# A hand-ordered opening for the first layer of a transformer stack: loads, norms, transposes, warm-up matmuls and zero fills

## The chip, the cores and the metric

The kernel runs on one core of one Trainium2 chip. The metric is the device time of the slowest (here the only) core in microseconds, us. Lower is better. A run of a one-core program is called fast when it lies within 1.5% of the fastest run of the same kernel. Runs of one kernel differ mostly by 1 to 2 us (about 0.1%). The changes discussed here are 1 to 8 us, so two measures stand side by side throughout: the time over several runs, and one instant read from the trace, at which the opening is over.

## The reference, cut to what matters

Two layers alternate, twice each: a sliding dilated attention (A) and a token-mixing MLP (B), on 2048 rows of 1024 columns in bf16.

```python
x = x + A(layernorm(x), wqkv, wo)      # first A: the part that the change touches
x = x + B(layernorm(x), w1, b1, w2, b2)
x = x + A(layernorm(x), wqkv, wo)
x = x + B(layernorm(x), w1, b1, w2, b2)
```

The first A begins with a layer norm of x, then `q, k, v = layernorm(x) @ wqkv`. The kernel computes v first ("the V matmuls": 16 row tiles x 2 column halves x 8 = 256 matmuls of 512 columns), then q and k ("the K/Q matmuls"). The biases b1 (3584 values) and b2 (2048 values) are wanted only by the first B, hundreds of us later.

## The kernel before

Each of the 16 row tiles is loaded, normed on VectorE (two half statistics, an aggregate, a rsqrt on ScalarE, the norm) and turned to its transpose hT, because the matmul wants the contraction on the partitions. The first four tiles are transposed by TensorE and copied by ScalarE; the others by DMA. Nobody orders the engines' queues by hand here: the code is traced in program order, and a scheduler decides the order of each engine's queue by what it believes will be ready first.

```python
def load_biases():
    with nc.allow_non_contiguous_dma(reason="tiny bias loads"):
        nc.gpsimd.dma_start(out=b1_bf[:], in_=B_b1.rearrange("(t p) -> p t", p=P))
        nc.gpsimd.dma_start(out=b2_bf[:], in_=B_b2.rearrange("(i m c) -> m i c", m=P, c=DIL))
    nc.vector.tensor_copy(out=b1_sb[:], in_=b1_bf[:])     # "the cast of b1"
    nc.vector.tensor_copy(out=b2_sb[:], in_=b2_bf[:])
...
for t in qT:                                              # zero fills, on GpSimd
    nc.gpsimd.memset(t[:, S:S + PAD], 0.0)
for t in Pm:
    nc.gpsimd.memset(t[0:HK, :, :, HW:KW], 0.0)
    nc.gpsimd.memset(t[HK:P, :, :, 0:HK], 0.0)
...
def prologue(c, i, on_pe):
    ...
    nc.sync.dma_start(out=x, in_=xin_v[c, i])
    yield
    mean, rs = stats(x, 1.0, eps1)
    norm_dve(x, x, mean, rs)
    if on_pe:
        tp = pss.tile([P, KD, P], BF16, name="s", tag="s")
        for kt in range(KD):
            nc.tensor.transpose(tp[:, kt, :], x[:, kt * P:(kt + 1) * P], ident[:])
        nc.scalar.copy(out=hT[:, :, cols(c, i)], in_=tp[:])
    else:
        nc.sync.dma_start_transpose(out=hT[:, :, cols(c, i)], in_=x)
    yield
...
    if first:
        pro = [prologue(c, i, c == 0 and i < 4) for c, i in order]
        ...                                               # loads of x and wv, interleaved
        wts = load_qk(0)
        load_biases()
        for k in range(4):
            next(pro[k])
            v_proj(v, *order[k], wv, (0,))
        ...                                               # other norms, other V matmuls
```

The cast turns the bf16 biases into the fp32 that later instructions want. b1 is read so that partition p gets elements p, p + 128, p + 256 and so on, which is 3584 separate pieces of 2 bytes; b2 is 1024 pieces of 4 bytes.

The softmax here doesn't subtract the row's maximum and nothing guards it: scores larger than these inputs give would overflow.

Of the kernel before, what the change touches and what calls it, by code (L numbers as in the profile page):

```python
# [9 lines left out]
ACT = mybir.ActivationFunctionType  # L10
ALU = mybir.AluOpType
FP32 = mybir.dt.float32
BF16 = mybir.dt.bfloat16

P = 128
# [10 lines left out]
def kernel(  # L26
# [15 lines left out]
    nc = tc.nc  # L42
    x_in = A_x[0]
    out2d = out[0]
    S, D = x_in.shape
    F = B_w1.shape[1]
    KD = D // P
    FT = F // P
    NT = S // P
# [4 lines left out]
    NDC = D // 512  # L54
    FB = 256
    NFB = F // FB
    GF = FB // P
    NW2 = 4
    HF = FT // NW2
    KW = P + W  # L60
    HK = P // 2
    HW = HK + W
    PAD = W
    SHIFT = 14.0
    assert D == H * DH and NT == 16 and NI == 8 and NG == 8 and HG == 4
    scale = float(DH) ** -0.5

    def pool(name, bufs, **kw):
        return ctx.enter_context(tc.tile_pool(name=name, bufs=bufs, **kw))
# [5 lines left out]
    gop = pool("gop", NFB)  # L75
# [5 lines left out]
    pss = pool("pss", 2, space=bass.MemoryType.PSUM)  # L81
    psa = pool("psa", 1, space=bass.MemoryType.PSUM)

    def m_tile():
        return psm.tile([P, 512], FP32, name="m", tag="m")
# [16 lines left out]
    def x2(name, shape=None, dt=BF16):  # L102
        return x2p.tile(shape or [P, D], dt, name=name, tag="x2")
# [4 lines left out]
    def st(name, shape):  # L108
        return stat.tile(shape, FP32, name=name, tag=name)
# [5 lines left out]
    ident = const.tile([P, P], BF16, name="ident")  # L115
    make_identity(nc, ident[:])
    eps1 = const.tile([P, 1], FP32, name="eps1")
# [20 lines left out]
# [4 lines that stand above are left out]
        nc.vector.tensor_copy(out=b1_sb[:], in_=b1_bf[:])  # L142
        nc.vector.tensor_copy(out=b2_sb[:], in_=b2_bf[:])

    hT = pers.tile([P, KD, S], BF16, name="hT")
    qT = [pers.tile([P, S + PAD], BF16, name=f"qT{n}") for n in range(2)]
    kT = [pers.tile([P, S], BF16, name=f"kT{n}") for n in range(2)]
    Pm = [pers.tile([P, HG, NI, KW], BF16, name=f"Pm{n}") for n in range(2)]
    for t in qT:
        nc.gpsimd.memset(t[:, S:S + PAD], 0.0)  # L150
    for t in Pm:
        nc.gpsimd.memset(t[0:HK, :, :, HW:KW], 0.0)
        nc.gpsimd.memset(t[HK:P, :, :, 0:HK], 0.0)

    xa = [dram.tile([S, D], BF16, name=f"xa{li}") for li in range(2)]
    xb = dram.tile([S, D], BF16, name="xb")
# [1 line left out]
    xin_v = x_in.rearrange("(i p c) d -> c i p d", p=P, c=DIL)  # L158
    out_v = out2d.rearrange("(i p c) d -> c i p d", p=P, c=DIL)
    wq_v = A_wqkv.rearrange("(kt p) c -> p kt c", p=P)  # L160
# [4 lines left out]
    def rows(t, c, i):  # L165
        return t[(c * NI + i) * P:(c * NI + i + 1) * P, :]

    def rsqrt(dst, var, mul, eps):
        ln = st("ln", [P, 1])
        nc.scalar.activation(out=ln[:], in_=var, func=ACT.Ln, bias=eps[:], scale=mul)  # L170
        nc.scalar.activation(out=dst, in_=ln[:], func=ACT.Exp, scale=-0.5)

    def stats(x, mul, eps):
        s = st("bn", [P, NDC, 6])
        for cc in range(NDC):
            nc.vector.bn_stats(out=s[:, cc, :], in_=x[:, cc * 512:(cc + 1) * 512])  # L176
        mv = st("mv", [P, 2])
        nc.vector.bn_aggr(out=mv[:], in_=s[:])  # L178
        rs = st("rs", [P, 1])
        rsqrt(rs[:], mv[:, 1:2], mul, eps)  # L180
        return mv[:, 0:1], rs

    def norm_dve(dst, x, mean, rs):
        nc.vector.tensor_scalar(out=dst, in0=x, scalar1=mean, scalar2=rs[:], op0=ALU.subtract, op1=ALU.mult)

    def norm_act(dst, x, mean, rs):
        bi = st("bi", [P, 1])
# [3 lines left out]
    def cols(c, i):  # L191
        return slice((c * NI + i) * P, (c * NI + i + 1) * P)

    def prologue(c, i, on_pe):
        t = gop.tile([P, GF, D], BF16, name="x0", tag="go") if i % 2 == 0 else prologue.t
        prologue.t = t
        x = t[:, i % 2, :]
        nc.sync.dma_start(out=x, in_=xin_v[c, i])
        yield
        mean, rs = stats(x, 1.0, eps1)  # L200
        norm_dve(x, x, mean, rs)
        if on_pe:
            tp = pss.tile([P, KD, P], BF16, name="s", tag="s")
            for kt in range(KD):
                nc.tensor.transpose(tp[:, kt, :], x[:, kt * P:(kt + 1) * P], ident[:])
            nc.scalar.copy(out=hT[:, :, cols(c, i)], in_=tp[:])  # L206
        else:
            nc.sync.dma_start_transpose(out=hT[:, :, cols(c, i)], in_=x)
        yield

    def load_wv():
        return [[wt_("wv", [P, KD // 2, 512]) for _ in range(2)] for _ in range(NDC)]

    def fill_wv(wv, n):
        for hf in range(2):
            nc.sync.dma_start(out=wv[n][hf][:],
                              in_=wq_v[:, hf * (KD // 2):(hf + 1) * (KD // 2), 2 * D + n * 512:2 * D + (n + 1) * 512])

    def v_proj(v, c, i, wv, ns):
        for n in ns:  # L220
            ps = m_tile()
            for kt in range(KD):
                nc.tensor.matmul(ps[:], lhsT=hT[:, kt, cols(c, i)], rhs=wv[n][kt // 4][:, kt % 4, :],  # L223
                                 start=(kt == 0), stop=(kt == KD - 1))
            nc.scalar.copy(out=v[c][i][:, n * 512:(n + 1) * 512], in_=ps[:])  # L225

    def load_qk(g2):
        ts = []
        for part in range(2):
            t = wt_("wqk", [P, KD, 256])  # L230
            nc.sync.dma_start(out=t[:], in_=wq_v[:, :, part * D + g2 * 256:part * D + (g2 + 1) * 256])
            ts.append(t)
        return ts
# [17 lines left out]
    def in_order(f, *args):  # L251
        with tc.issue_after(last_pe[0].ins) if last_pe[0] is not None else nullcontext():
            last_pe[0] = f(*args)
# [88 lines left out]
    order = [(c, i) for c in range(DIL) for i in range(NI)]  # L342
# [72 lines left out]
    for li in range(2):  # L415
        first = li == 0
        v = [[None] * NI for _ in range(DIL)]
        for c, i in order:
            v[c][i] = vhp.tile([P, D], BF16, name="v", tag="vh")
        wv = load_wv()  # L420
        if first:
            pro = [prologue(c, i, c == 0 and i < 4) for c, i in order]
            next(pro[0])
            next(pro[1])
            fill_wv(wv, 0)
            next(pro[2])
            next(pro[3])
            fill_wv(wv, 1)
            for p_ in pro[4:]:
                next(p_)  # L430
            wts = load_qk(0)
            load_biases()
            for k in range(4):
                next(pro[k])
                v_proj(v, *order[k], wv, (0,))
            for k in range(4, NT):
                next(pro[k])
            for k in range(4):
                v_proj(v, *order[k], wv, (1,))
            for k in range(4, NT):  # L440
                v_proj(v, *order[k], wv, (0, 1))
            res = lambda c, i: xin_v[c, i]
        else:
            fill_wv(wv, 0)
            fill_wv(wv, 1)
            wts = load_qk(0)
            for i in range(NI):
                for c in range(DIL):
                    v_proj(v, c, i, wv, (0, 1))
            res = lambda c, i: rows(xb, c, i)  # L450
        oT = [gop.tile([P, S], BF16, name="oT", tag="go") for _ in range(NG)]
        h2 = [[None] * NI for _ in range(DIL)]
        chunks = [(0, 0), (0, 1), (1, 0), (1, 1)]
        last_pe[0] = None
        for part, n in chunks:
            in_order(qk_chunk, 0, wts, part, n)
        wo = None
        for vis in range(2 * NU):
            u, b = divmod(vis, 2)
            if b == 0 and u + 1 < NU and (u + 1) % (2 * DIL) == 0:  # L460
                wts = load_qk((u + 1) // (2 * DIL))
            if vis == 2 * NU - 6:
                wo = load_wo()
            in_order(scores, u, b)
            for n in range(2):
                if n and vis:
                    in_order(values, *divmod(vis - 1, 2), v, oT)
                if u + 1 < NU:
                    in_order(qk_chunk, u + 1, wts, *chunks[2 * b + n])
                else:  # L470
                    in_order(out_proj, 0, 2 * b + n, oT, wo, res, xa[li], h2)
        in_order(values, NU - 1, 1, v, oT)
        for c, i in order[4:]:
            out_proj(c, i, oT, wo, res, xa[li], h2)
        g = [None] * NFB
        for fb in range(NFB):
            gemm1(fb, h2, g)
        if first:
            ln_exp_table()
        for i in range(NI):  # L480
            w2t = load_w2(i)
            for c in range(DIL):
                gemm2(c, i, w2t, g, xa[li], rows(xb, c, i) if first else out_v[c, i], first)
# [30 lines left out]
```

## Time and profile before

| | before |
|---|---|
| time, median of 3 runs | 1308.38 us (1307.17 to 1308.64) |
| TensorE busy, share of the span | 99% |
| first K/Q matmul (all 256 V matmuls done) | 72.93 us |
| 256 V matmuls at 6.91 us per 32 | 55.3 us |
| loss in the opening, the difference | 17.6 us |

The page of the kernel before gives busy time, share of the span and number of instructions of each engine:

```profile
PE 1289.1 (99%) x9376; PEld 581.1 (44%) x9376; DVE 388.1 (30%) x646; ACT 384.0 (29%) x622; POOL 11.6 (1%) x19
```

TensorE (PE) is the limit of the whole kernel, and a gain can come only from its first 73 us. In the chain of waits that ended last (start us, duration us, what), the opening and the first long pieces are:

```profile
2.75 7.57 DMA x<-in_A_x_dram
20.86 52.07 PE m L223 x240
72.93 6.91 PE m L240 x32
```

The chain begins with the loads of x; from 20.86 us on TensorE never waits again until the K/Q matmuls begin at 72.93 us. **This instant, the first K/Q matmul in the chain of waits, is the measure used below.** (The timeline shows the same matmul 0.16 us earlier, at 72.77 us, while it lets the stretch of V matmuls end at 72.94: its stretches overlap. Some of the expectations quoted below use that figure.)

The timeline (start us, duration us, engine, line, operation, out<-in, count, and in brackets the idle time before it and what ended it) shows what the first 20 us are made of:

```profile
4.07 1.88 DVE L176 BATCH_NORM_STATS2 bn<-x 128x6 f32<-128x512 bf16 x3 [3.00 <-DMA x<-in_A_x_dram]
...
6.65 1.63 DVE L184 TENSOR_SCALAR x<-x,mv,rs 128x1024 bf16<-128x1024 bf16 x1
8.03 1.99 POOL L153 MEMSET Pm<- 64x2048 bf16 x1
...
8.99 1.32 DVE L184 TENSOR_SCALAR x<-x,mv,rs 128x1024 bf16<-128x1024 bf16 x1 [0.60 <-ACT rs L171]
9.97 1.68 POOL L140 DMA_DIRECT2D b_bf<-in_B_b_dram  x1
...
12.80 0.99 ACT L206 COPY hT<-s 128x1024 bf16<-128x1024 bf16 x1
...
13.85 5.24 PE L223 MATMUL m<-wv,hT 128*128 128x512 bf16 x16 [2.46 <-ACT hT L206]
...
20.77 0.17 DVE L142 CAST b_sb<-b_bf 128x28 f32<-128x28 bf16 x1
```

Tile 0 has landed at 4.07 us. Its norm takes 1.63 us and tile 1's 1.32 us (later ones 0.53) while GpSimd (POOL) is at its fills. Each of the two norms ends 0.28 or 0.29 us after the fill beside it does (8.28 and 8.00 us, 10.31 and 10.02 us). The fills also keep GpSimd from issuing the b1 load before 9.97 us, and the cast of b1 (20.77) comes when the first five tiles are through VectorE. The first V matmul starts at 13.85 us. The first of them start 0.43 us apart, from 17.20 us on it is 0.216 us; below, the first state is called half rate, or a cold array.

### The profile page before, as it was taken

Reading aid. Unit: us, or ns where it says so; the run is one execution under the profiler, and the core shown is the slowest. Engines: PE = TensorE matmul, PEld = TensorE weight load, DVE = VectorE, ACT = ScalarE, POOL = GpSimd, SP = SyncE. Lnnn points to the kernel's source line nnn. Section 1 sums busy time; section 2 is a strip of 40 time slices with the busy share of each in tenths; the row PEclk is TensorE's granted clock in tenths of the full one; section 3 lists DMA queues with packets and bytes.
Section 4 is the critical chain, followed back from the end, with each engine's and each line's share of the span. In section 5 each row is a group of like instructions: output and inputs, shape, how many; then the busy total and the mean of one; then the engine's idle time right before and its main releaser. Section 6 shows DMA issues by size and latency. Waiting matters only on the chain.

```text
span 1305.9 us, 20991 instructions
## 1 busy us (share of the span) xinstructions
PE 1289.1 (99%) x9376; PEld 581.1 (44%) x9376; DVE 388.1 (30%) x646; ACT 384.0 (29%) x622; POOL 11.6 (1%) x19
## 2 busy tenths in 40 slices
PE   6999999999999999999999999999999999999998
PEld 2444444444444444444444444444444444444443
DVE  7136667830000013223210566688000000111111
ACT  4347776531111110000023676764211111000000
POOL 3000000000000000000000000000000000000000
PEclk9999999999999999999999999999999999999999
DMA  9521112452322227456431100144522222334320
GB/s 246 125 66 34 34 34 83 150 165 69 94 65 76 72 71 166 122 137 171 121 89 41 54 23 18 34 130 153 145 65 81 81 59 73 109 105 134 116 91 33
DMA packets 192202, 121.96 MB, mean 93 GB/s; under 512 B 34416, under 2 KB 173680, under 8 KB 192112
## 3 DMA queue, kind: packets, MB, share of 16 engines
q1 hardware_dynamic: 192000, 120.61, 33.0%
q8 instruction: 73, 1.20, 0.4%
q0 software_dynamic: 112, 0.01, 0.1%
q14 instruction: 17, 0.14, 0.0%
HBM read 96.48 MB, written 16.78 MB: 87 GB/s over the span
## 4 chain that ended last, share of the span: by engine, by line
PE 97%; DVE 1%; DMA 1%; ACT 0%; issue 0%; SPq 0%
PE m L240 18%; PE s L403 15%; PE s L360 15%; PE m L223 9%; PE m L403 7%; PE m L360 7%; PE acc L360 7%; PE acc L403 7%; PE m L333 7%; PE acc L294 1%; PE s L266 1%; PE acc L298 1%; DMA x<-in_A_x_dram 1%; DVE bn L176 0%; DVE xn L335 0%; PE acc L290 0%
## 5 line engine op out<-in xcount | busy, mean ns | idle before, releaser
L360 PEld LDWEIGHTS <-w 128*128 128x128 bf16 x1792 | 175.4, 98 | 211.4
L403 PEld LDWEIGHTS <-w 128*128 128x128 bf16 x1792 | 175.3, 98 | 211.5
L240 PE MATMUL m<-hT,wqk 128*128 128x512 bf16 x1024 | 241.8, 380 | 0.0
L360 PE MATMUL s<-h,w 128*128 128x512 bf16 x896 | 202.8, 379 | 0.0
L403 PE MATMUL s<-g,w 128*128 128x512 bf16 x896 | 199.9, 379 | 0.0
L406 DVE SCALAR_TENSOR_TENSOR xo<-s,b_sb,xs 128x512 bf16<-128x512 f32 x32 | 24.0, 751 | 540.7 <-PE s L403 536.5
L240 PEld LDWEIGHTS <-wqk 128*128 128x128 bf16 x1024 | 90.6, 98 | 108.6 <-issue 12.9
L223 PE MATMUL m<-wv,hT 128*128 128x512 bf16 x512 | 112.7, 383 | 3.3 <-ACT hT L206 3.3
L275 DVE TENSOR_TENSOR Pm<-pc,band 64x1152 bf16<-64x1152 bf16 x128 | 96.2, 752 | 65.1 <-ACT pc L270 63.1
L333 PE MATMUL m<-wo,oT 128*128 128x512 bf16 x512 | 112.2, 379 | 0.1
L270 ACT ACTIVATE pc<-s,shift 128x576 bf16<-128x576 f32 x128 | 87.8, 737 | 59.9 <-PE s L266 59.9
L360 PE MATMUL acc<-h,w 128*128 128x512 bf16 x448 | 103.9, 379 | 0.0
L403 PE MATMUL acc<-g,w 128*128 128x512 bf16 x448 | 100.6, 379 | 0.0
L403 PE MATMUL m<-g,w 128*128 128x512 bf16 x448 | 99.3, 379 | 0.0
L360 PE MATMUL m<-h,w 128*128 128x512 bf16 x448 | 99.0, 379 | 0.0
L170 ACT ACTIVATE ln<-mv,eps 128x1 f32<-128x1 f32 x64 | 18.9, 295 | 235.2 <-DVE mv L178 235.0
L367 ACT ACTIVATE g<-s,b_sb 128x1024 bf16<-128x1024 f32 x28 | 31.2, 1114 | 166.9 <-PE s L360 166.9
L223 PEld LDWEIGHTS <-hT 128*128 128x128 bf16 x512 | 50.2, 99 | 65.1 <-ACT hT L206 3.8
L333 PEld LDWEIGHTS <-oT 128*128 128x128 bf16 x512 | 49.4, 98 | 59.7 <-issue 1.3
L225 ACT CAST v<-m 128x512 bf16<-128x512 f32 x64 | 37.4, 585 | 64.3 <-PE m L223 64.3
L312 DVE TENSOR_TENSOR oT<-acc,rd 128x512 bf16<-128x512 f32 x64 | 44.0, 687 | 39.7 <-ACT rd L310 39.7
L246 DVE CAST qT<-m 128x512 bf16<-128x512 f32 x32 | 21.8, 682 | 95.3 <-PE m L240 95.3
(54 smaller groups left out, 582.2 us busy)
## 6 DMA issues: line engine op xcount, KB each, us to landing
w<-in_B_w_dram SPq DMA_DIRECT2D x56, 512.0 KB, 3.8
w<-in_B_w_dram SPq DMA_DIRECT2D x64, 448.0 KB, 4.6
wqk<-in_A_wqkv_dram SPq DMA_DIRECT2D x16, 512.0 KB, 5.6
xa<-xn SPq DMA_DIRECT2D x32, 256.0 KB, 2.0
xs<-xa SPq DMA_DIRECT2D x32, 256.0 KB, 3.2
x<-in_A_x_dram SPq DMA_DIRECT2D x16, 256.0 KB, 8.4
wv<-in_A_wqkv_dram SPq DMA_DIRECT2D x8, 512.0 KB, 6.3
wo<-in_A_wo_dram SPq DMA_DIRECT2D x8, 512.0 KB, 3.5
```

Source lines behind the costliest of these rows:

```text
L223: nc.tensor.matmul(ps[:], lhsT=hT[:, kt, cols(c, i)], rhs=wv[n][kt // 4][:, kt % 4, :], start=(kt == 0), stop=(kt == KD - 1))
L225: nc.scalar.copy(out=v[c][i][:, n * 512:(n + 1) * 512], in_=ps[:])
L240: mm = nc.tensor.matmul(ps[:], lhsT=wts[part][:, kt, (g % 2) * P:(g % 2 + 1) * P], rhs=hT[:, kt, lo:lo + 512], start=(kt == 0), stop=(kt = ...
L246: nc.vector.tensor_copy(out=dst[:, lo:lo + 512], in_=ps[:])
L270: nc.scalar.activation(out=pc[:, 2 * n:2 * n + 2].rearrange("p h t k -> p h (t k)"), in_=ss[n][:, :, 0:HB * HW], func=ACT.Exp, scale=scale ...
L275: nc.vector.tensor_tensor(out=pm[rp, :, b * HB:(b + 1) * HB, r * HK:r * HK + HW], in0=pc[rp], in1=mk, op=ALU.mult)
L312: nc.vector.tensor_tensor(out=oT[g][:, lo:lo + hb * P], in0=acc[:, 0, :], in1=rd[:], op=ALU.mult)
L333: mm = nc.tensor.matmul(ps[:], lhsT=oT[g][:, cols(c, i)], rhs=wo[n][g // 4][:, g % 4, :], start=(g == 0), stop=(g == NG - 1))
L360: nc.tensor.matmul(pairs[fl][0][dc], lhsT=wt[c][:, i, fl * P:(fl + 1) * P], rhs=h2[c][i][:, dc * 512:(dc + 1) * 512], start=(k == 0), stop ...
L367: nc.scalar.activation(out=g[fb][:, fl, :].rearrange("p (n d) -> p n d", n=2), in_=t[:], func=ACT.Gelu_apprx_tanh, bias=b1_sb[:, ft:ft + 1])
L403: nc.tensor.matmul(aps[dc], lhsT=w2t[ft // HF][:, ft % HF, c::DIL], rhs=g[ft // GF][:, ft % GF, dc * 512:(dc + 1) * 512], start=(ft == 0), ...
L406: nc.vector.scalar_tensor_tensor(out=xo[:, dc * 512:(dc + 1) * 512], in0=aps[dc], scalar=b2_sb[:, i, c:c + 1], in1=xs[:, dc * 512:(dc + 1) ...
```

## The change

The intent: start the V matmuls earlier and keep TensorE at full rate. Each engine's queue of the opening is written down by hand and chained with `issue_after`, which fixes the issue order on one engine and adds no wait. Tile 0 is loaded and normed in halves, the copies to hT are made in halves, one more tile is transposed on TensorE, 14 matmuls of zeros are to wake the array, and the zero fills go to VectorE, behind its last norm.

```diff
-    for t in qT:
-        nc.gpsimd.memset(t[:, S:S + PAD], 0.0)
-    ...
+    def zero_fill():
+        for t in qT:
+            nc.vector.memset(t[:, S:S + PAD], 0.0)
+        ...
+    def chain_(eng, f, *args):
+        with tc.issue_after(last[eng].ins) if eng in last else nullcontext():
+            last[eng] = f(*args)
+    def start_up(v, wv):
+        np_ = 5
+        warm = x2("warm", [P, 512])
+        nc.vector.memset(warm[:], 0.0)
+        ...          # S_ half statistics, A_ aggregate, R_ rsqrt, N_ norm, tr transposes on TensorE,
+        ...          # C_ copy to hT, V_ V matmuls, E_ copy of v out of PSUM, T_ transpose by DMA
+        for _ in range(14):
+            chain_("PE", lambda: nc.tensor.matmul(wm[:], lhsT=warm[:, 0:P], rhs=warm[:], start=True, stop=True))
+        chain_("SP", x_load, 0, halves)
+        chain_("SP", x_load, 1)
+        chain_("SP", w_load, 0, 0)
+        chain_("SP", w_load, 0, 1)
+        chain_("SP", x_load, 2)
+        ...
+        pe = [(tr, 0), (V_, 0, 0, lo4), (tr, 1), (V_, 0, 0, hi4), (V_, 1, 0, lo4), (tr, 2), (V_, 1, 0, hi4),
+              (V_, 2, 0, a8), (V_, 0, 1, a8), (tr, 3), (V_, 1, 1, a8), (V_, 2, 1, a8), (tr, 4)]
+        pe += [(V_, k, n, a8) for k in range(3, NT) for n in range(NDC)]
+        act = [(R_, 0), (C_, 0), (R_, 1), (C_, 1), (R_, 2), (E_, 0, 0), (C_, 2), (R_, 3), (E_, 1, 0), (R_, 4),
+               (E_, 2, 0), (C_, 3), (E_, 0, 1), (R_, 5), (E_, 1, 1), (R_, 6), (C_, 4), (E_, 2, 1), (R_, 7)]
+        es = [(E_, k, n) for k in range(3, NT) for n in range(NDC)]
+        for j, e in enumerate(es):
+            act.append(e)
+            if j + 8 < NT:
+                act.append((R_, j + 8))
+        dve = [(S_, 0, 0), (S_, 0, 1), (A_, 0)]
+        for k in range(NT):
+            nx = k + 1 < NT
+            if nx:
+                dve.append((S_, k + 1, 0))
+            dve.append((N_, k, halves if k == 0 else whole))
+            if nx:
+                dve += [(S_, k + 1, 1), (A_, k + 1)]
+        dve.append((zero_fill,))
+        ...
     if first:
-        pro = [prologue(c, i, c == 0 and i < 4) for c, i in order]
-        ...
+        start_up(v, wv)
         wts = load_qk(0)
         load_biases()
-        ...
```

`load_biases()` is still called, and is not part of any chain.

More of the change, by code (lines that the diff above doesn't have):

```diff
@@ L148 @@
     Pm = [pers.tile([P, HG, NI, KW], BF16, name=f"Pm{n}") for n in range(2)]
-    for t in qT:
-        nc.gpsimd.memset(t[:, S:S + PAD], 0.0)
-    for t in Pm:
-        nc.gpsimd.memset(t[0:HK, :, :, HW:KW], 0.0)
-        nc.gpsimd.memset(t[HK:P, :, :, 0:HK], 0.0)
+    def zero_fill():
+        for t in qT:
+            nc.vector.memset(t[:, S:S + PAD], 0.0)
+        for t in Pm:
+            nc.vector.memset(t[0:HK, :, :, HW:KW], 0.0)
+            r = nc.vector.memset(t[HK:P, :, :, 0:HK], 0.0)
+        return r
     xa = [dram.tile([S, D], BF16, name=f"xa{li}") for li in range(2)]
@@ L170, in rsqrt @@
         nc.scalar.activation(out=ln[:], in_=var, func=ACT.Ln, bias=eps[:], scale=mul)
-        nc.scalar.activation(out=dst, in_=ln[:], func=ACT.Exp, scale=-0.5)
+        return nc.scalar.activation(out=dst, in_=ln[:], func=ACT.Exp, scale=-0.5)
     def stats(x, mul, eps):
@@ L183, in norm_dve @@
     def norm_dve(dst, x, mean, rs):
-        nc.vector.tensor_scalar(out=dst, in0=x, scalar1=mean, scalar2=rs[:], op0=ALU.subtract, op1=ALU.mult)
+        return nc.vector.tensor_scalar(out=dst, in0=x, scalar1=mean, scalar2=rs[:], op0=ALU.subtract, op1=ALU.mult)
     def norm_act(dst, x, mean, rs):
@@ L192, in cols @@
         return slice((c * NI + i) * P, (c * NI + i + 1) * P)
-    def prologue(c, i, on_pe):
-        t = gop.tile([P, GF, D], BF16, name="x0", tag="go") if i % 2 == 0 else prologue.t
-        prologue.t = t
-        x = t[:, i % 2, :]
-        nc.sync.dma_start(out=x, in_=xin_v[c, i])
-        yield
-        mean, rs = stats(x, 1.0, eps1)
-        norm_dve(x, x, mean, rs)
-        if on_pe:
-            tp = pss.tile([P, KD, P], BF16, name="s", tag="s")
-            for kt in range(KD):
-                nc.tensor.transpose(tp[:, kt, :], x[:, kt * P:(kt + 1) * P], ident[:])
-            nc.scalar.copy(out=hT[:, :, cols(c, i)], in_=tp[:])
-        else:
-            nc.sync.dma_start_transpose(out=hT[:, :, cols(c, i)], in_=x)
-        yield
+    last = {}
@@ new lines, in chain_, with x_load, w_load, S_ @@
+    def chain_(eng, f, *args):
[5 more added lines that the diff above has]
+        nc.vector.memset(warm[:], 0.0)
+        xs, tps, pss_, mvs, sts, rss = {}, {}, {}, {}, {}, {}
+        def x_load(k, hs=(slice(0, D),)):
+            c, i = order[k]
+            if k % 2 == 0:
+                x_load.t = gop.tile([P, GF, D], BF16, name="x0", tag="go")
+            xs[k] = x_load.t[:, k % 2, :]
+            for h in hs:
+                r = nc.sync.dma_start(out=xs[k][:, h], in_=xin_v[c, i][:, h])
+            return r
+        def w_load(n, hf):
+            return nc.sync.dma_start(out=wv[n][hf][:], in_=wq_v[:, hf * (KD // 2):(hf + 1) * (KD // 2),
+                                                                2 * D + n * 512:2 * D + (n + 1) * 512])
+        def S_(k, cc):
+            if cc == 0:
+                sts[k] = st("bn", [P, NDC, 6])
+            return nc.vector.bn_stats(out=sts[k][:, cc, :], in_=xs[k][:, cc * 512:(cc + 1) * 512])
+        def A_(k):
+            mvs[k] = st("mv", [P, 2])
+            return nc.vector.bn_aggr(out=mvs[k][:], in_=sts[k][:])
+        def R_(k):
+            rss[k] = st("rs", [P, 1])
+            return rsqrt(rss[k][:], mvs[k][:, 1:2], 1.0, eps1)
+        def N_(k, hs):
+            for h in hs:
+                r = norm_dve(xs[k][:, h], xs[k][:, h], mvs[k][:, 0:1], rss[k])
+            return r
+        def tr(k):
+            tps[k] = pss.tile([P, KD, P], BF16, name="s", tag="s")
+            for kt in range(KD):
+                r = nc.tensor.transpose(tps[k][:, kt, :], xs[k][:, kt * P:(kt + 1) * P], ident[:])
+            return r
+        def C_(k):
+            for hf in range(2):
+                ks = slice(hf * KD // 2, (hf + 1) * KD // 2)
+                r = nc.scalar.copy(out=hT[:, ks, cols(*order[k])], in_=tps[k][:, ks, :])
+            return r
+        def V_(k, n, kts):
+            if kts[0] == 0:
+                pss_[k, n] = m_tile()
+            for kt in kts:
+                r = nc.tensor.matmul(pss_[k, n][:], lhsT=hT[:, kt, cols(*order[k])], rhs=wv[n][kt // 4][:, kt % 4, :],
+                                     start=(kt == 0), stop=(kt == KD - 1))
+            return r
+        def E_(k, n):
+            c, i = order[k]
+            return nc.scalar.copy(out=v[c][i][:, n * 512:(n + 1) * 512], in_=pss_[k, n][:])
+        def T_(k):
+            return nc.sync.dma_start_transpose(out=hT[:, :, cols(*order[k])], in_=xs[k])
+        wm = m_tile()
+        for _ in range(14):
+            chain_("PE", lambda: nc.tensor.matmul(wm[:], lhsT=warm[:, 0:P], rhs=warm[:], start=True, stop=True))
+        halves = (slice(0, D // 2), slice(D // 2, D))
+        whole = (slice(0, D),)
+        chain_("SP", x_load, 0, halves)
[3 more added lines that the diff above has]
+        chain_("SP", x_load, 2)
+        chain_("SP", x_load, 3)
+        chain_("SP", w_load, 1, 0)
+        chain_("SP", w_load, 1, 1)
+        for k in range(4, NT):
+            chain_("SP", x_load, k)
+        lo4, hi4 = range(KD // 2), range(KD // 2, KD)
+        a8 = range(KD)
+        pe = [(tr, 0), (V_, 0, 0, lo4), (tr, 1), (V_, 0, 0, hi4), (V_, 1, 0, lo4), (tr, 2), (V_, 1, 0, hi4),
[17 more added lines that the diff above has]
+        dve.append((zero_fill,))
+        sp = [(T_, k) for k in range(np_, NT)]
+        qs = {"PE": pe, "ACT": act, "DVE": dve, "SP": sp}
+        need = {R_: lambda k: k in mvs, N_: lambda k, h: k in rss, tr: lambda k: (N_, k) in done, C_: lambda k: k in tps,
+                V_: lambda k, n, kts: ((C_, k) in done or (T_, k) in done), E_: lambda k, n: (V_, k, n) in done,
+                T_: lambda k: (N_, k) in done}
+        done = set()
+        while any(qs.values()):
+            for eng, q in qs.items():
+                while q and (q[0][0] not in need or need[q[0][0]](*q[0][1:])):
+                    f, *args = q.pop(0)
+                    chain_(eng, f, *args)
+                    if f is V_:
+                        if args[2][-1] == KD - 1:
+                            done.add((f, args[0], args[1]))
+                    elif args:
+                        done.add((f, args[0]))
@@ L421 @@
         if first:
-            pro = [prologue(c, i, c == 0 and i < 4) for c, i in order]
-            next(pro[0])
-            next(pro[1])
-            fill_wv(wv, 0)
-            next(pro[2])
-            next(pro[3])
-            fill_wv(wv, 1)
-            for p_ in pro[4:]:
-                next(p_)
+            start_up(v, wv)
             wts = load_qk(0)
             load_biases()
-            for k in range(4):
-                next(pro[k])
-                v_proj(v, *order[k], wv, (0,))
-            for k in range(4, NT):
-                next(pro[k])
-            for k in range(4):
-                v_proj(v, *order[k], wv, (1,))
-            for k in range(4, NT):
-                v_proj(v, *order[k], wv, (0, 1))
             res = lambda c, i: xin_v[c, i]
```

## The prediction

> **What bounds it now.** One core, 1308.4 us. TensorE is busy 99% of the span at a granted clock of 0.999, and 97% of the chain that ended last is TensorE: 6.91 us per 32 matmuls of 512 columns, 0.216 us each. The change touches only the opening; by the instruction order TensorE's stream is unchanged after that. So what counts is when the 256 V matmuls end: 72.9 us now (chain of waits). 256 x 0.216 = 55.3 us, so 17.6 us of the opening are loss. By the timeline:
> - to 4.07: x0 lands.
> - 4.07 to 13.85: statistics, norm, transpose, copy. Two VectorE norms take 1.63 and 1.32 us against 0.53 later, while GpSimd runs 1.8 us fills. The first copy to hT waits behind tile 2's rsqrt until 12.80; its transposes ended at 9.4.
> - 13.85 to 17.2: 0.43 us per matmul, then 0.216. The Trainium skill ("TensorE: Matmul & The Clock Gate", Part 1) says an idle array runs at half rate for about 3.4 us; this trace agrees. About 1.7 us.
> - 18.9 to 20.86: transposes 2 and 3 and their copy. Then nothing waits: 240 matmuls in 52.07 us.
>
> **The change, were nothing in its way.** x0's halves land near 3.8; aggregate 5.2, norm 6.0 (0.3 us per half, fills gone from GpSimd), first V near 7.3 instead of 13.85, warm (14 zero matmuls from 1.2 to 6). Transposes 1 and 2 leave gaps of 0.6 to 1 us. 16 V done near 12.6, the other 240 take 51.8, transposes 3 and 4 1.1: V ends near 65.5. Gain 7 us. Later DMA transposes (1.9 us of queue each, one needed per 3.45) keep up; VectorE's fills come after the last norm.
>
> **What is in its way.** Nothing orders the bias loads. In the changed order GpSimd issues the b1 load near 1.1 us (before: 9.97), and VectorE's cast of b1 stands between tile 0's second statistics and its aggregate; before it came after tile 7's first. So tile 0 waits until b1 has landed. That load took 9.9 us from issue to landing before, its queue's first packets 5 us after the issue; while they moved (15 to 19 us) traffic fell from 370 to 60 GB/s. The skill ("DMA: Bandwidth & Descriptors", table at the start) gives a first byte of about 1 us for this path; this trace shows 5, on busy engines. Early there is less traffic, so I estimate landing between 7 and 11 us, middle 9.3: aggregate 9.4 instead of 5.2. The dummies end 4 us before the first transpose, so half of their worth is lost (+1 us). First V near 11.7, V ends near 70.5. The b2 cast (before tile 2's aggregate) should cost little. Net gain 2 us; with b1 landing at 11.5, a loss of 1.
>
> **Prediction.** 1306.0 us, 8 in 10 between 1301.5 and 1309.5. Within 2%: 0.98; faster: 0.01; slower: 0.01.
>
> **What would show it.**
> - VectorE idle before the b1 cast or the aggregate, released by the b1 load: 3 us or more (my step); near 0 (the full 7 us).
> - Norms of tiles 0 and 1 at 0.55 us per 1024 columns.
> - First V near 11.7, at 0.43 or 0.216 us each.
> - First K/Q matmul near 70.7 instead of 72.9; later work only shifted.
>
> **What would make it wrong.** b1 landing by 5 us (1301.5) or after 12; its small packets delaying x1 and wv; late DMA transposes.

## The result

| | before | changed |
|---|---|---|
| time, median of 4 runs each, same rounds | 1308.06 us (1307.17 to 1308.64) | 1309.30 us (1308.38 to 1310.03) |
| ratio of fast runs, 95% interval | | 1.001 (0.9992 to 1.0027) |
| first K/Q matmul | 72.93 us | 73.75 us |
| span of the profiled run | 1305.9 us | 1306.7 us |

Ratios here and below are the mean time of one kernel's fast runs over that of the other's of the same rounds, so not quite the ratio of the medians quoted. By time the two kernels are the same (what counts is whether the interval holds 1). By the traces the whole difference is in the opening: first K/Q comes 0.82 us later, and the span is 0.8 us longer.

The chain of waits of the changed kernel, in place of the one shown above:

```profile
1.37 8.74 DMA b_bf<-in_B_b_dram
45.97 27.79 PE m L255 x128
73.75 6.91 PE m L350 x32
```

The chain no longer begins with x. It begins with the load of a bias, which took 8.74 us and which nothing in this layer uses. The timeline shows how that load came onto the path:

```profile
1.37 1.68 POOL L140 DMA_DIRECT2D b_bf<-in_B_b_dram  x1 [0.27 <-issue]
...
3.04 1.29 DVE L224 BATCH_NORM_STATS2 bn<-x 128x6 f32<-128x512 bf16 x2 [1.71 <-DMA x<-in_A_x_dram]
...
10.13 0.18 DVE L142 CAST b_sb<-b_bf 128x28 f32<-128x28 bf16 x1 [5.81 <-DMA b_bf<-in_B_b_dram]
10.22 0.20 DVE L228 BATCH_NORM_AGGREGATE mv<-bn 128x2 f32<-128x12 f32 x1
...
11.03 0.74 DVE L186 TENSOR_SCALAR x<-x,mv,rs 128x512 bf16<-128x512 bf16 x2
...
11.50 1.03 PE L242 MATMUL s<-ident,x 128*128 128x128 bf16 x8 [4.85 <-DVE x L186]
...
12.57 1.07 ACT L248 COPY hT<-s 128x512 bf16<-128x512 bf16 x2 [1.58 <-PE s L242]
...
13.21 1.89 PE L255 MATMUL m<-wv,hT 128*128 128x512 bf16 x4 [0.68 <-ACT hT L248]
```

GpSimd, rid of its fills, issues the b1 load at 1.37 us instead of 9.97. VectorE's cast of b1 (L142) stands between tile 0's statistics and its aggregate (L228), and VectorE is idle for 5.81 us until b1 has landed. Norms are quick now (0.74 us for tile 0's two halves, 0.55 for tile 1), as intended. The copy of tile 0 begins only after all eight transposes, at 12.57 us. The first V matmuls run at half rate again: 1.89 us for 4.

The early load did a second thing. The windows view (stretch in us, length, busy time and instructions of PE, PEld, DVE, ACT and POOL, granted TensorE clock, share of the 16 DMA engines, GB/s moved) shows the stretch from 6 to 10 us, first in the kernel before, then in the changed one:

```profile
6.00:10.00 4.00, 1.04 (x8) 0.77 (x8) 3.36 (x5) 0.99 (x4) 3.91 (x4) 1.00 1.02 351
```

```profile
6.00:10.00 4.00, 0.65 (x4) 0.10 (x1) 0.00 (x0) 0.00 (x0) 0.00 (x0) 0.88 1.28 101
```

The DMA engines are fully busy in both, but moved 351 GB/s before and 101 GB/s after. By the trace's count of packets by queue, the software queue (GpSimd's, only biases) moved 112 packets, 0.01 MB, most of them between 5 and 10 us; in the kernel before the same packets moved between 15 and 19 us. Tile 2 of x lands near 12.2 us instead of 10.35.

There is a third item, after 28 us. VectorE and ScalarE in the changed kernel:

```profile
31.30 0.20 ACT L173 ACTIVATE rs<-ln 128x1 f32<-128x1 f32 x1
31.41 0.57 ACT L261 CAST v<-m 128x512 bf16<-128x512 f32 x1
31.54 0.55 DVE L186 TENSOR_SCALAR x<-x,mv,rs 128x1024 bf16<-128x1024 bf16 x1
32.00 0.69 DVE L224 BATCH_NORM_STATS2 bn<-x 128x6 f32<-128x512 bf16 x1
...
32.72 0.21 DVE L228 BATCH_NORM_AGGREGATE mv<-bn 128x2 f32<-128x12 f32 x1
...
32.97 0.29 ACT L172 ACTIVATE ln<-mv,eps 128x1 f32<-128x1 f32 x1 [0.98 <-DVE mv L228]
```

Rsqrt (ends at 31.50), norm (L186), second half statistics (L224), aggregate (L228), and the next rsqrt at 32.97: a loop of 1.99 us from one rsqrt to the next (30.98 to 32.97). ScalarE's fixed order puts one copy of V (L261) between two rsqrts, so the copies come every 1.99 us, while TensorE needs only 1.73 us for 8 matmuls. The copies empty PSUM, so TensorE should have to wait for them. The profile names no such wait; e3 tests it. In the kernel before the scheduler had put the statistics of the next tile ahead of the norm, and V's copies kept TensorE's pace (240 V matmuls in 52.07 us, in the chain above).

### The profile page after: what moved, and what is told of

Read it like the earlier page. It is cut to its first block, busy times and chain, and to the rows that moved or that the text cites. A ratio compares the mean times of both kernels' runs of the same rounds, so it can differ in the third digit from the quotient of the medians.

```text
span 1306.7 us, 21044 instructions
## 1 busy us (share of the span) xinstructions
PE 1294.7 (99%) x9398; PEld 583.0 (45%) x9398; DVE 392.6 (30%) x654; ACT 385.1 (29%) x628; POOL 4.3 (0%) x13
## 4 chain that ended last, share of the span: by engine, by line
PE 95%; DVE 2%; ACT 1%; DMA 1%; issue 0%; POOL 0%; POOLq 0%
PE m L350 18%; PE s L513 15%; PE s L470 15%; PE m L513 7%; PE m L470 7%; PE acc L470 7%; PE acc L513 7%; PE m L443 7%; PE m L333 4%; PE m L255 3%; PE acc L404 1%; PE s L376 1%; PE acc L408 1%; DMA b_bf<-in_B_b_dram 1%; DVE xn L445 1%; DVE x L186 0%
## 5 line engine op out<-in xcount | busy, mean ns | idle before, releaser
L445 DVE TENSOR_TENSOR xn<-m,xr 128x512 bf16<-128x512 f32 x64 | 44.0, 688 | 8.0 <-PE m L443 6.6
```

What stands on the lines that cost most here:

```text
L445: nc.vector.tensor_tensor(out=xn[:, xs_], in0=ps[:], in1=xr[:, xs_], op=ALU.add)
```

## The experiments

Three suspects, then: the cast in VectorE's queue (the wait), the bias packets on the DMA engines (the traffic), the loop. Twelve kernels ran, in three calls; the kernel before ran again in each (medians 1307.84, 1307.97 and 1308.33 us). All results were within tolerance.

| run | first K/Q, us | time, us | ratio to before (95%) |
|---|---|---|---|
| before | 72.93 | 1308.06 | |
| changed | 73.75 | 1309.30 | 1.0010 (0.9992 to 1.0027) |
| e1_casts_late | 73.39 | 1308.15 | 1.0004 (0.9989 to 1.0019) |
| e2_loads_late | 68.68 | 1304.19 | 0.9970 (0.9956 to 0.9984) |
| e3_stats_ahead | 74.13 | 1308.39 | 1.0003 (0.9989 to 1.0017) |
| e4_all_three | 67.76 | 1302.37 | 0.9959 (0.9946 to 0.9971) |
| e5_before_fills | 75.75 | 1310.31 | 1.0021 (1.0007 to 1.0035) |
| e6_before_bias_late | 72.93 | 1307.53 | 0.9996 (0.9982 to 1.0010) |
| e7_few_packets | 71.13 | 1305.00 | 0.9973 (0.9958 to 0.9988) |
| e8_reordered | 65.85 | 1300.48 | 0.9942 (0.9930 to 0.9955) |
| e9_no_dummies | 67.63 | 1302.06 | 0.9951 (0.9935 to 0.9968) |
| e10_fills_back | 67.51 | 1302.75 | 0.9957 (0.9943 to 0.9972) |
| e11_after_no_dummies | 75.17 | 1309.65 | 1.0011 (0.9996 to 1.0026) |
| e12_after_36_dummies | 74.35 | 1308.88 | 1.0004 (0.9989 to 1.0019) |

### e1: the wait alone taken away

```diff
-        nc.vector.tensor_copy(out=b1_sb[:], in_=b1_bf[:])
-        nc.vector.tensor_copy(out=b2_sb[:], in_=b2_bf[:])
+        with tc.issue_after(last["DVE"].ins):
+            nc.vector.tensor_copy(out=b1_sb[:], in_=b1_bf[:])
+            nc.vector.tensor_copy(out=b2_sb[:], in_=b2_bf[:])
```

> The changed kernel with one edit: VectorE's two bias casts are queued after its last work of the opening; the bias loads on GpSimd stay as early as they were (issue near 1.4 us). My theory (the cast of b1 holds tile 0 until 10.1 us): the aggregate of tile 0 comes near 4.4 us instead of 10.2, and the first V matmul near 7.6 instead of 13.2. But the small packets of the bias loads still move from 5 to 10 us, so the second half of wv (11.6 us in the changed kernel) and tile 2 of x (12.2 us) land as late as before, and the first K/Q matmul comes near 70.8 us instead of 73.75 (about 3 us gained, not 6). Rival A (the cast is the whole loss): first K/Q near 67.5. Rival B (the cast only stands where another wait would be, the chain of norms or the copies being the limit anyway): first K/Q at 73 or later.

First K/Q came at 73.39 us, 0.36 us earlier than in the changed kernel. That is what rival B forecast (73 or later): another wait stood behind the cast. It was not one of those that rival B named, the norms or the copies. The timeline of e1:

```profile
4.38 0.21 DVE L229 BATCH_NORM_AGGREGATE mv<-bn 128x2 f32<-128x12 f32 x1
...
7.37 1.04 PE L256 MATMUL m<-wv,hT 128*128 128x512 bf16 x4 [0.68 <-ACT hT L249]
...
8.03 0.20 ACT L174 ACTIVATE rs<-ln 128x1 f32<-128x1 f32 x1
12.24 0.69 DVE L225 BATCH_NORM_STATS2 bn<-x 128x6 f32<-128x512 bf16 x1 [5.15 <-DMA x<-in_A_x_dram]
...
13.44 1.03 PE L243 MATMUL s<-ident,x 128*128 128x128 bf16 x8 [5.03 <-DVE x L187]
```

The aggregate comes at 4.38 and the first V matmul at 7.37 us, as expected. But then VectorE is idle for 5.15 us until tile 2 has landed at 12.24, and the transposes of tile 1 wait until 13.44. Tile 1's rsqrt was done at 8.23. The hand-made order has tile 2's first statistics ahead of tile 1's norm, so the norm waits for a load that it does not need. I had missed this step, and so expected 3 us. (No run has this order changed with the early bias load kept, so what the order alone would give back is not shown.)

### e2: the wait and the traffic taken away

```diff
+        with tc.issue_after(last["DVE"].ins):
+            nc.vector.memset(b1_bf[:], 0.0)     # the load must wait for this fill,
+            nc.vector.memset(b2_bf[:], 0.0)     # which VectorE does at the end of the opening
         (casts as in e1)
```

> As e1, and the bias loads themselves are made late as well (a VectorE fill of their tiles at the end of the opening, which the loads must wait for). My theory: without the small packets between 5 and 10 us, traffic in that stretch is near 350 GB/s instead of 80 to 140, wv's second half lands near 9 and tile 2 of x near 10 us, and first K/Q comes near 68.5 us, 2 us or more ahead of e1. Rival (the bias traffic costs nothing, only the wait does): e2 equals e1 within 0.5 us.

First K/Q at 68.68 us, as expected, and 4.7 us ahead of e1. The stretch from 6 to 10 us and tile 2's statistics in e2:

```profile
6.00:10.00 4.00, 2.02 (x14) 0.76 (x12) 2.27 (x6) 1.47 (x4) 0.00 (x0) 1.00 1.02 341
```

```profile
9.06 0.69 DVE L228 BATCH_NORM_STATS2 bn<-x 128x6 f32<-128x512 bf16 x1 [1.69 <-DMA x<-in_A_x_dram]
...
10.26 0.62 PE L246 MATMUL s<-ident,x 128*128 128x128 bf16 x8 [1.57 <-DVE x L190]
```

341 GB/s instead of 101 (131 in e1), tile 2 at 9.06 us instead of 12.24, the transposes of tile 1 at 10.26 instead of 13.44. That is 3.2 of the 4.7 us. The rest comes right after, at half rate: after the 5.03 us of idle time in e1, TensorE's 8 transposes took 1.03 us and the next 8 V matmuls 3.62, in e2 0.62 and 1.89. So the early bias load did its harm on two parallel ways: the wait of the cast (until 10.1 us) and the late landing of tile 2 (12.2 us). Taking away the first alone only uncovered the second, a little longer one. With both gone the change is worth 4.25 us (72.93 less 68.68).

### e3 and e4: the loop

```diff
-            if nx:
-                dve.append((S_, k + 1, 0))
-            dve.append((N_, k, halves if k == 0 else whole))
-            if nx:
-                dve += [(S_, k + 1, 1), (A_, k + 1)]
+            ahead = [(S_, k + 1, 0), (S_, k + 1, 1), (A_, k + 1)] if nx else []
+            norm = [(N_, k, halves if k == 0 else whole)]
+            dve += ahead + norm if k >= 4 else ahead[:1] + norm + ahead[1:]
```

e3 is the changed kernel with this edit alone; e4 is e2 with it.

> The changed kernel with one edit, the bias casts left where they are: from tile 4 on VectorE takes the statistics and the aggregate of the next tile before the norm of this one. Theory: in the changed kernel ScalarE's fixed order couples one copy of V to one rsqrt, and the rsqrt of tile k+1 waits on VectorE for norm k, half of the statistics and the aggregate of k+1, a loop of 1.99 us that is longer than the 1.73 us of 8 matmuls; 8 to 10 groups between 28 and 46 us lose 0.26 us each. The edit takes the norm out of the loop: groups at 1.73 us, first K/Q near 71.9 instead of 73.75. Rival (these gaps are late DMA transposes or loads): unchanged at 73.5 or later.

> The changed kernel with all three edits: casts late, bias loads late, statistics ahead of norms. If the three losses are the whole of what kept the gain away, first K/Q near 67 us (before: 72.93) and the time about 6 us under that of before (1302.3). If the losses overlap (the second hides behind the first), 68 to 69.

The long stretch of V matmuls after tile 4's transposes, in the changed kernel and in e3 (timeline, TensorE only):

```profile
27.33 46.42 PE L255 MATMUL m<-wv,hT 128*128 128x512 bf16 x208
```

```profile
28.99 45.14 PE L255 MATMUL m<-wv,hT 128*128 128x512 bf16 x203
```

The same stretch in e2 and in e4:

```profile
22.26 46.42 PE L259 MATMUL m<-wv,hT 128*128 128x512 bf16 x203
```

```profile
22.62 45.14 PE L259 MATMUL m<-wv,hT 128*128 128x512 bf16 x203
```

In both pairs the stretch shrank by the same 1.28 us (the count of 203 against 208 is the trace's; a few records are missing), so the loop is real. It was expected to be worth about 1.9 us. Yet e3's first K/Q came later, at 74.13, a miss by 2.2 us: b1 landed later in that run (first transpose at 12.27 instead of 11.50 us), and the array stayed at half rate for longer (the 8 V matmuls after the second transposes took 3.44 us against 1.95). In e4, where neither disturbs, the same edit brought 0.92 us (68.68 to 67.76); there tile 2 landed at 9.42 us instead of e2's 9.06, which is the missing 0.36. The size of the loop is therefore 1.28 us. e4 came out at 1302.37 us against the 1302.3 expected, at the better end of my two figures for the time and in between for first K/Q (67 and 68 to 69).

### e5: the fills alone moved

The kernel before, with only the fills moved behind VectorE's last norm:

```diff
-    for t in qT:
-        nc.gpsimd.memset(t[:, S:S + PAD], 0.0)
-    ...
+    def zero_fill(): ...                # the same fills on VectorE
...
+            with tc.issue_after(last_norm[0].ins):
+                zero_fill()
```

> The kernel before with one part of the change alone: the zero fills go from GpSimd to VectorE, after its last norm. Nothing else is ordered by hand. In the built order this alone puts the bias loads early on GpSimd and the cast of b1 between the first two statistics on VectorE. Theory (the fills were what kept the bias loads out of the way): b1's load is issued near 1.4 us and lands between 10 and 11, tile 0's aggregate comes near 11 instead of 5.9, tile 2 lands near 12.2 instead of 10.35, and first K/Q is near 74.5 us against 72.93 before, although the norms of tiles 0 and 1 take 0.55 us instead of 1.63 and 1.32. Rival (the harm comes from the hand-made order, not from the fills): first K/Q at 72.4 or earlier.

```profile
1.37 1.68 POOL L140 DMA_DIRECT2D b_bf<-in_B_b_dram  x1 [0.27 <-issue]
...
11.75 0.18 DVE L142 CAST b_sb<-b_bf 128x28 f32<-128x28 bf16 x1 [6.88 <-DMA b_bf<-in_B_b_dram]
...
13.83 0.55 DVE L185 TENSOR_SCALAR x<-x,mv,rs 128x1024 bf16<-128x1024 bf16 x1
```

First K/Q at 75.75 us: 2.8 us later than before, where 1.6 were expected. The ratio is 1.0021 with an interval above 1. The fills had been a plug: no line of the kernel says so, but while GpSimd was busy with them until 10 us, the scheduler put the bias loads, and with them the cast, behind the opening. Moving them gave the norms their 0.55 us back and cost VectorE 6.88 us of idle time. The hand-made order of the change has no part in this.

### e6: the bias traffic moved away in the kernel before

```diff
+        nc.vector.memset(b1_bf[:], 0.0)
+        nc.vector.memset(b2_bf[:], 0.0)
...
-            load_biases()
...
+            with tc.issue_after(last_norm[0].ins):
+                load_biases()
```

> The kernel before with the bias loads and casts made late, fills left on GpSimd. In that kernel the small packets move from 15 to 19 us, after the first four tiles have landed. Theory: nothing on the path waits for what they delay, so first K/Q stays at 72.9 within 0.3 us and the time is the same. Rival (bias traffic costs about 4 us wherever it is, as e2 against e1 gained 4.7): first K/Q near 69 to 70.

First K/Q at 72.93 us, to the hundredth as before. The same packets between 15 and 19 us cost, by these two traces, no more than about 0.1 us (the last 240 V matmuls take 51.97 us instead of 52.07, and start 0.10 us later), since by then nothing on the path waits for a load. In this kernel the traffic has no price of its own; its price is set by who waits.

### e7: the same early load in few pieces

```diff
-            nc.gpsimd.dma_start(out=b1_bf[:], in_=B_b1.rearrange("(t p) -> p t", p=P))
-            nc.gpsimd.dma_start(out=b2_bf[:], in_=B_b2.rearrange("(i m c) -> m i c", m=P, c=DIL))
+            nc.gpsimd.dma_start(out=b1_bf[:], in_=B_b1.rearrange("(p t) -> p t", p=P))
+            nc.gpsimd.dma_start(out=b2_bf[:], in_=B_b2.rearrange("(m i c) -> m i c", m=P, c=DIL))
```

This puts the biases at wrong places. (It stayed within tolerance all the same, since the biases are only of the order of 0.001.)

> Wrong result on purpose: the changed kernel, order untouched (cast of b1 still ahead of tile 0's aggregate), but each partition reads its biases as one contiguous run, 128 runs of 56 bytes for b1 instead of 3584 of 2 bytes, and 128 of 32 bytes for b2 instead of 1024 of 4. Theory (the number of tiny pieces is what makes the load slow and starves the others): b1 lands by about 5 us, tile 0's aggregate near 5.3, traffic between 6 and 10 us stays near 340 GB/s, tile 2 lands near 9, and first K/Q comes near 69 us, within 1 us of e2 (68.5). Rival (the software queue is slow by itself, whatever it carries): b1 still lands at 8 us or later and first K/Q at 71.5 or later.

```profile
5.00 0.16 DVE L142 CAST b_sb<-b_bf 128x28 f32<-128x28 bf16 x1
...
10.46 0.69 DVE L224 BATCH_NORM_STATS2 bn<-x 128x6 f32<-128x512 bf16 x1 [2.95 <-DMA x<-in_A_x_dram]
```

```profile
6.00:10.00 4.00, 2.18 (x16) 0.94 (x13) 1.47 (x4) 1.47 (x4) 0.00 (x0) 1.00 1.01 295
```

b1's cast runs at 5.00 us, right behind tile 0's statistics and without any wait, in the same place of the queue and from the same issue at 1.37 us. b1 landed 3.2 us after its issue, against 8.7 in the changed kernel. So the software queue is not slow by itself; for b1 it was the number of pieces. (b2, contiguous too, still took 6.6 us, against 7.2; why is not shown.) Traffic is 295 GB/s instead of 101. First K/Q at 71.13 us is 2.6 us better than the changed kernel and 2.4 worse than e2, where within 1 us was expected. Tile 2 came only at 10.46 us (e2: 9.06, e4: 9.42), probably because of the 128 pieces of 32 bytes for b2 and of 56 for b1, since nothing else on the DMA engines was changed against e2. And after an idle time of TensorE of 2.80 us (e2: 1.57) the next V matmuls fell to half rate (8 in 3.21 us against 1.89 in e2).

### e8: a better version

```diff
 (e4, and:)
-        for _ in range(14):
+        for _ in range(11):
-        chain_("SP", w_load, 0, 1)
         chain_("SP", x_load, 2)
+        chain_("SP", w_load, 0, 1)
-        act = [(R_, 0), (C_, 0), (R_, 1), (C_, 1), (R_, 2), (E_, 0, 0), ...
+        act = [(R_, 0), (C_, 0), (R_, 1), (C_, 1, (0,)), (R_, 2), (C_, 1, (1,)), (E_, 0, 0), ...
-            dve += ahead + norm if k >= 4 else ahead[:1] + norm + ahead[1:]
+            dve += ahead + norm if k >= 4 else ahead[:1] + norm + ahead[1:] if k else norm + ahead
```

> Attempt at a better version: e4 with the queues of the first tiles reordered. Tile 2 of x is loaded before wv's second half; VectorE does norm 0 before the statistics of tile 1 (which wait for its load); the rsqrt of tile 2 goes between the halves of tile 1's copy; 11 dummies instead of 14. In e4 the transposes of tiles 1 and 2 start at 10.62 and 13.41. Expected: near 8.8 and 11.2, first K/Q near 65.8 instead of 67.59, time near 1300.6. If the loads are the limit and not the order, first K/Q stays at 67 or later.

```profile
7.37 1.04 PE L259 MATMUL m<-wv,hT 128*128 128x512 bf16 x4 [0.68 <-ACT hT L252]
9.08 0.62 PE L246 MATMUL s<-ident,x 128*128 128x128 bf16 x8 [0.68 <-DVE x L190]
...
11.39 0.62 PE L246 MATMUL s<-ident,x 128*128 128x128 bf16 x8
...
20.70 45.14 PE L259 MATMUL m<-wv,hT 128*128 128x512 bf16 x208
65.68 7.07 PE L352 MATMUL m<-hT,wqk 128*128 128x512 bf16 x32
```

Transposes 1 and 2 at 9.08 and 11.39 us, first K/Q at 65.85 us in the chain (65.68 in the timeline), 1300.48 us: the expectation held to 0.3 us. Against the kernel before that is 7.1 us of opening, ratio 0.9942. This version beats both kernels, by 0.6 to 0.7%. Which of its four edits over e4 brought the last 1.9 us was not separated.

### e9 and e10: what the dummies and the fills are worth in e8

e9 is e8 without the 11 zero matmuls and their tile; e10 is e8 with the fills back on GpSimd.

> e8 without its 11 zero matmuls. Theory (they are worth what the cold array costs, some 3.4 us at 0.43 us per matmul instead of 0.216): the first V matmuls run at 0.43 us, first K/Q near 67.3 us instead of 65.68, time about 1.6 us above e8. Rival (nothing in the first 12 us waits for TensorE's speed): first K/Q within 0.3 us of e8.

> e8 with the zero fills back on GpSimd, bias loads and casts still late. Theory (GpSimd's fills slow VectorE's norms, 1.63 and 1.32 us in the kernel before against 0.55): norms 0 and 1 take about 1 us longer together with the chain behind them, first K/Q near 67.2 us instead of 65.68. Rival (the norms have slack): within 0.3 us of e8.

In e9 the first V matmuls take 0.43 us each again, and tile 2 lands at 8.52 us (7.88 in e8). In e10 VectorE's norm of tile 1 is slow again:

```profile
7.35 1.89 PE L257 MATMUL m<-wv,hT 128*128 128x512 bf16 x4 [0.68 <-ACT hT L250]
...
8.52 0.69 DVE L226 BATCH_NORM_STATS2 bn<-x 128x6 f32<-128x512 bf16 x1 [1.17 <-DMA x<-in_A_x_dram]
```

```profile
8.66 1.46 DVE L188 TENSOR_SCALAR x<-x,mv,rs 128x1024 bf16<-128x1024 bf16 x1
```

First K/Q came at 67.63 us without the dummies (1.78 us later than e8) and at 67.51 with the fills back (1.66 us later). Both parts of the change pay once the bias load is out of their way, but these single traces do not give each part's exact size. In e9, 0.64 of the 1.78 us is the later landing of tile 2, for which the transposes of tile 1 wait; some 1.1 us is left for the cold array. (The median times, 1302.06 and 1300.48 us, differ by 1.6.) In e10 tile 0's norm was hardly slower (0.79 us for its halves); 1.1 us of the 1.66 stand at the transposes of tile 1 (10.17 instead of 9.08), 0.93 of it in the norm, and 0.5 us is one later wait for a DMA transpose, which is not shown to come from the fills. The slow norm ends at 10.12 us, again 0.28 us after a fill (9.84).

### e11 and e12: the dummies in the changed kernel

e11 is the changed kernel without its 14 zero matmuls, e12 with 36 of them.

> The changed kernel as it was, without its 14 zero matmuls. They end near 6.6 us, its first transpose starts at 11.50, and its first V matmuls run at 0.43 us anyway. Theory (by then the array is at half rate again, the dummies are worth nothing): first K/Q stays at 73.75 within 0.5 us. Rival (half their worth is kept, as predicted): first K/Q 0.8 us or more later.

> The changed kernel with 36 zero matmuls instead of 14, so that they last until about 11 us and the first transposes find a warm array. Theory: the first transposes and V matmuls run at full rate, but between them stand the norms, copies and tile 2's load (12.2 us), so only 0.5 to 1 us comes of it: first K/Q near 73.0. Rival (the cold array is the main loss of the changed kernel): 2 us or more, 71.7 or earlier.

Raw first K/Q: 75.17 and 74.35, against 73.75 with 14 dummies. Neither is as expected, because b1's landing differs from run to run: the cast came at 11.07 and 10.98 us instead of 10.13. From the first transpose (12.43, 12.34, 11.50 us) to first K/Q it is 62.74, 62.01 and 62.25 us. So the 14 dummies are worth about 0.5 us there, and warm transposes about 0.2 us more; but a single trace each, with a moving landing, does not fix such small figures, and the times (1309.65 and 1308.88 us) do not separate them. It is clear only that the cold array was not the main loss of the changed kernel (rival of e12: 2 us or more).

## Why the prediction was right or wrong

The time (1309.3 us) lies in the range (1301.5 to 1309.5), near its upper end, and "within 2%" was right. The middle of the forecast, a gain of 2 us, did not come: the measured difference is about +1 us with an interval that includes none. So the direction was missed, and that the range of 8 us still held the result, by 0.2 us, owes something to luck. "Within 2%" was safe from the start: all that the opening loses is 17.6 us, 1.3% of the time.

- **Fills and norms: right.** Norms of 0.55 us, seen; e10 shows what a slow one costs.
- **The cast of b1 holds tile 0: right in mechanism, and seen in the chain of waits.** VectorE idle 5.81 us (3 or more was said), b1 landed at 10.1 us (7 to 11 was said, middle 9.3), aggregate at 10.22 (9.4). But it was the only way of harm that the forecast priced, and it is not the only one: with the cast out of the way (e1) only 0.36 us came back. The forecast price of the early load, 5.0 us (65.5 to 70.5), fits the 5.1 measured for cast and traffic together.
- **"The dummies end 4 us before the first transpose, so half of their worth is lost (+1 us)": roughly right.** They end at 6.65 us, the first transpose starts at 11.50, the first V matmuls run at 0.43 us. The comparison with e11 leaves them about 0.5 us, the e8 and e9 pair 1.1 to 1.8 us where they work.
- **First V near 11.7: 1.5 us too early (13.21).** 0.8 us is the landing. The rest is the way from the aggregate to the first V matmul, sized at 2.3 us, measured 3.0: ScalarE's first half copy waited for all eight transposes, which ran at 0.13 us each on the cold array.
- **"Later DMA transposes keep up": true of the transposes, but the step was incomplete.** The loop of rsqrt, norm, statistics and aggregate (1.99 us against 1.73) was not seen; it costs 1.28 us. With the landing (0.8) and the slower start (0.7) this is 2.8 of the 3.2 us between the predicted end of V (70.5) and the measured one (73.75), if the three may be added, which no run shows.
- **The small packets "delaying x1 and wv": named as a risk, not priced.** They hit tile 2 of x, and e1 against e2 shows that this way is as long as the wait of the cast. The harm of the early bias load is 5.1 us together (73.75 less 68.68); taking away the wait alone (e1) gives back 0.36 us. The traffic alone was not taken away; e7, which takes most of both, gives back 2.6.
- **"Were nothing in its way ... V ends near 65.5": too rosy for the change as written.** With the bias load gone it is 68.68 (e2), with the loop gone 67.76 (e4). 65.85 was reached only after reordering the queues around tile 2's load (e8).

What stays open: how long the bias load takes was between 8.7 us (changed kernel) and 10.4 us (e5) from issue to landing, and why it varies was not looked into.

## What to carry to other kernels

Before moving work off an engine, ask what that work was holding back: an idle engine will issue its next loads early, and the consumer of those loads may be put into the middle of a queue that matters. When queues are ordered by hand, order everything that the stage touches, also what "does not belong to it", and look in the built order for a wait on a foreign load. Many tiny pieces harm most when the first loads of a kernel are on their way; load them late, or in contiguous runs. And when taking away one wait gives nothing, look for a second one of the same length behind it before dropping the theory.

## What the Trainium skill lacked or had wrong

- "DMA: Bandwidth & Descriptors", "Specifications": a first byte after about 1 us for the GpSimd path. Here b1 was issued at 1.37 us, and the trace counts the first packets of that queue between 5 and 6 us. Other traffic alone does not explain it: in e7, issued at the same 1.37 us but in contiguous runs, the first packets are counted between 2.4 and 3 us. The page does not say by how much this figure grows with the number of pieces.
- The same page, "Rules for kernel authors", says that a non-contiguous last dimension becomes one descriptor per element, and "Specifications" that transfers under 512 bytes fall short of the full rate. The first is not shown here, since the trace counts packets (112 for both biases) and not descriptors; the low rate agrees with the second. What the page lacks is the size of the harm to others: 112 packets with 0.01 MB of biases brought the traffic of all queues from 341 GB/s (e2) to 131 (e1) and 101 GB/s (changed kernel) from 6 to 10 us, and contiguous runs (e7) to 295 GB/s.
- "GPSIMD Engine Reference", section 1, says that GpSimd shares its SBUF interfaces with VectorE and that some VectorE modes contend. The trace agrees, and gives the size that this section lacks: a norm of 128 x 1024 took 1.63, 1.32 (before) or 1.46 us (e10) beside a fill, and 0.53 to 0.55 otherwise. All three ended 0.28 or 0.29 us after the fill. Not every VectorE instruction was held up: three statistics beside a fill took 1.88 us together (at 4.07 us), as many as three took without one (1.88 at 10.35).
- "TensorE: Matmul & The Clock Gate", Part 1, agrees on the half rate and its length (0.43 us, then 0.216 us per matmul after about 3.4 us). The granted clock in a profile can miss it: between 14 and 16 us the kernel before shows a granted clock of 1.00 while its matmuls took 0.43 us, whereas the changed kernel shows 0.50 between 12 and 14 us. This is no gap in the skill: the same Part 1 warns not to trust the recorded clock events fully.
